# Retention and SwiGLU on one core: the first two chunks as pairs of batches, and an FFN that starts on half of its tokens

## The chip, the core and the metric

The kernel runs on one core of a Trainium2 chip, from one launch. The metric is the device time of that core in microseconds (us); lower is better. Of the two timed runs of the kernel before, one took 251.46 us and one, which was disturbed, 474.38 us; the comparisons in this document leave disturbed runs out. The profile is one execution of the same program, with a span of 248.7 us.

A core has four engines that matter here. TensorE multiplies matrices and writes its results to PSUM, a small memory of eight banks. VectorE and ScalarE read PSUM and write SBUF, the working memory. GpSimd works on SBUF alone, and can also issue transfers that change the type on the way. Sixteen DMA engines carry the transfers.

## What is computed

The inputs q, k and v have 4 batches, 8 heads, 768 positions and 64 numbers a head. The first half of the reference is a recurrence over the positions:

```python
gamma = 1.0 - 2.0 ** (-5.0 - np.arange(H))
for t in range(S):
    state = gamma * state + k[t] (outer) v[t]      # 64x64 for each batch and head
    y[:, :, t] = scale * q[t] @ state
```

Then the 8 heads of a position are laid side by side, which makes 3072 tokens of 512 numbers, and each token goes through a gated FFN with inner width 1536:

```python
rms = np.sqrt(np.mean(x * x, axis=-1, keepdims=True) + 1e-06)
xn = x / rms * rms_g
g = xn @ w_gate
silu = g * (1.0 / (1.0 + np.exp(-g)))
val = xn @ w_val
return silu * val @ w_out
```

The kernels don't step through the positions one by one. They cut the 768 positions into six chunks of 128. Inside a chunk the scores q k are multiplied by a causal mask and applied to v; what came earlier enters through the state, which is carried from chunk to chunk. The decay is folded into a factor on v and one on y.

## The kernel before

Six chunks follow one another. While the FFN of chunk c runs on all 512 tokens of the four batches, the attention of chunk c + 1 is worked off in slots between its matmuls. Each batch has its pieces: transposes (t), scores (a), y, norm (n) and transposes of the normed tokens (x).

The order of the first chunk is written out, and the FFN starts when all four batches are through it:

```python
for step in ("C0 T0 V0 W0 A0 T1 V1 Y0 W1 A1 T2 V2 Y1 W2 N0 A2 T3 X0 V3 Y2 W3 S0 N1 A3 S1 X1 Y3 N2 X2 S2").split():
    P[step[0]](0, int(step[1]))
...
warm_up(3)
piece_s(3)
piece_n(0, 3)
piece_x(0, 3)
warm_up(2)
```

The inputs of a batch and chunk come with one position on a partition, so a row of a transfer is 64 numbers of four bytes. Most are loaded by the sync queue as float32 and cast on GpSimd; those of chunk 0, batches 1 to 3, are cast in the transfer:

```python
x = loads.tile([128, H, D], F32, name=name)
i = nc.sync.dma_start(out=x, in_=src[b].rearrange("h (c p) d -> c p h d", p=C)[c])
...
nc.gpsimd.tensor_copy(qb, q_f.rearrange("p h d -> p (h d)"))
nc.gpsimd.tensor_copy(kb, k_f.rearrange("p h d -> p (h d)"))
nc.gpsimd.tensor_tensor(out=vp, in0=v_f, in1=vdec[:, c, :, None].to_broadcast([128, H, D]), op=ALU.mult)
```

From chunk 2 on, q and k are transposed by DMA, before that by TensorE. The scores and y of one batch:

```python
for hp in range(NHP):                      # 4 pairs of heads
    for i in range(2):
        r = slice(i * 64, i * 64 + 64)
        nc.tensor.matmul(a_ps[i][:, hp, :], d["kT"][r, hp, :], d["qT"][r, hp, :], start=True, stop=True)
for i in range(2):
    nc.vector.tensor_tensor(out=am[:, i], in0=a_ps[i], in1=causal..., op=ALU.mult)
...
# y: 8 matmuls of 64 columns, then the state part: 4 of 128 columns
nc.tensor.matmul(y_ps[:, h, :], d["am"][:, i, hp, :], d["vp"][:, h, :], ...)
nc.tensor.matmul(y_ps[:, 2 * hp:2 * hp + 2, :], d["qT"][:, hp, :], st_b[b][:, hp, :], ...)
# the addition to the state: 4 of 128 columns
nc.tensor.matmul(kv_ps[:, hp, :], d["kb"][:, sl], d["vp"][:, 2 * hp:2 * hp + 2, :], start=True, stop=True)
```

After these, VectorE scales y (x), ScalarE squares it, GpSimd adds and takes the power -0.5 (ms, rstd), VectorE norms (xn), and TensorE or a DMA transposes. The FFN, with four PSUM banks (fps) of its own:

```python
def gv(n):                                 # n of 12: 8 matmuls of 512 columns
    for s in range(KS):
        nc.tensor.matmul(g_ps, wg_b[:, s, sl], xnT[:, s, :], start=s == 0, stop=s == KS - 1)
    for s in range(KS):
        nc.tensor.matmul(v_ps, wv_b[:, s, sl], xnT[:, s, :], start=s == 0, stop=s == KS - 1)
    nc.scalar.activation(sg, g_ps, AF.Silu)
    nc.vector.tensor_tensor(out=hT[:, n, :], in0=sg, in1=v_ps, op=ALU.mult)

def down(b, n0=0, n1=NFF):                 # 12 matmuls of 512 columns for a batch
    for n in range(n0, n1):
        nc.tensor.matmul(o_ps, hT[:, n, b * C:(b + 1) * C], wo_b[:, n, :], ...)
    nc.scalar.copy(o_sb, o_ps)
    nc.sync.dma_start(out=out_v[c, b], in_=o_sb)
```

Of the kernel before, what the change touches and what calls it, by code (L numbers as in the profile page):

```python
# [11 lines left out]
AX = mybir.AxisListType  # L12
# [5 lines left out]
def kernel(  # L18
# [15 lines left out]
    C = 128  # L34
# [11 lines left out]
    loads = ctx.enter_context(tc.tile_pool(name="loads", bufs=8))  # L46
    work = ctx.enter_context(tc.tile_pool(name="work", bufs=3))
    ffw = ctx.enter_context(tc.tile_pool(name="ffw", bufs=3))
    aps = ctx.enter_context(tc.tile_pool(name="aps", bufs=4, space=bass.MemoryType.PSUM))
    fps = ctx.enter_context(tc.tile_pool(name="fps", bufs=4, space=bass.MemoryType.PSUM))  # L50


    out_v = out.rearrange("(b c p) m -> c b p m", b=B, p=C)

    SYNC_DEP = mybir.DependencyInfo(mybir.DependencyClass.Sync, mybir.DependencyReason.DATA)


    raw = {}

    def load(c, b, after=None):  # L60
        t = []
        for name, src in (("q_f", q), ("k_f", k), ("v_f", v)):
            x = loads.tile([128, H, D], F32, name=name)
            i = nc.sync.dma_start(
                out=x, in_=src[b].rearrange("h (c p) d -> c p h d", p=C)[c])
            if after is not None:
                tc.add_manual_dep(i.ins, after.ins.name, SYNC_DEP, reason="transfer order")
            t.append(x)
        raw[c, b] = t

    raw0 = {}

    def load0(b):
        for name, src in (("qb", q), ("kb", k)):
            x = work.tile([128, DM], BF16, name=name, bufs=6)
            nc.gpsimd.dma_start(
                out=x.rearrange("p (h d) -> p h d", h=H),
                in_=src[b].rearrange("h (c p) d -> c p h d", p=C)[0])  # L80
            raw0[name, b] = x
        x = loads.tile([128, H, D], F32, name="v_f")
        nc.gpsimd.dma_start(out=x, in_=v[b].rearrange("h (c p) d -> c p h d", p=C)[0])
        raw0["v", b] = x

    load(0, 0)
    g_col = const.tile([128, KS], F32, name="g_col")
    with nc.allow_non_contiguous_dma(reason="one column per 128 entries"):
        nc.scalar.dma_start(out=g_col, in_=moe_rms_g.rearrange("(s p) -> p s", p=128))


    pos_i = const.tile([128, NCH], mybir.dt.int32, name="pos_i")
    nc.gpsimd.iota(pos_i, pattern=[[C, NCH]], base=1, channel_multiplier=1)

    lngs = const.tile([128, H], F32, name="lngs")
    for h in range(H):
# [5 lines left out]
    pos_f = const.tile([128, NCH], F32, name="pos_f")  # L102
    nc.vector.tensor_copy(pos_f, pos_i)
    darg = const.tile([128, NCH, H], F32, name="darg")
    nc.vector.tensor_tensor(
        out=darg, in0=pos_f[:, :, None].to_broadcast([128, NCH, H]),
        in1=lngs[:, None, :].to_broadcast([128, NCH, H]), op=ALU.mult)
    vdec = const.tile([128, NCH, H], F32, name="vdec")
    ydec = const.tile([128, NCH, H], F32, name="ydec")
    nc.scalar.activation(vdec, darg, AF.Exp, scale=-1.0, bias=zero)  # L110
    nc.scalar.activation(ydec, darg, AF.Exp, scale=1.0, bias=lnscale)

    warm = const.tile([128, 1], F32, name="warm")
    nc.scalar.activation(warm, zero, AF.Silu)
    mhalf = const.tile([128, 1], F32, name="mhalf")
    nc.vector.memset(mhalf, -0.5)
    ident = const.tile([128, 128], BF16, name="ident")
    make_identity(nc, ident)
    causal = const.tile([128, 128], BF16, name="causal")
    nc.gpsimd.memset(causal, 1.0)  # L120
    nc.gpsimd.affine_select(
        out=causal, in_=causal, compare_op=ALU.is_ge, fill=0.0, base=0,
        pattern=[[1, 128]], channel_multiplier=-1)
    for b in range(1, B):
        load0(b)

    g_bc = const.tile([128, DM], F32, name="g_bc")

    st_f = [const.tile([128, NHP, 2 * D], F32, name=f"st_f{b}") for b in range(B)]
    st_b = [const.tile([128, NHP, 2 * D], BF16, name=f"st_b{b}") for b in range(B)]
    for b in range(B):
        nc.vector.memset(st_b[b], 0.0)


    wg_b = const.tile([128, KS, DFF], BF16, name="wg_b")
    wv_b = const.tile([128, KS, DFF], BF16, name="wv_b")
    wo_b = const.tile([128, NFF, DM], BF16, name="wo_b")
    wg_v = moe_w_gate.rearrange("(k p) n -> p k n", p=128)  # L140
    wv_v = moe_w_val.rearrange("(k p) n -> p k n", p=128)
    wo_v = moe_w_out.rearrange("(n p) m -> p n m", p=128)
    WB = 384

    landed = {}

    def load_w(i):
        sl = slice(i * WB, (i + 1) * WB)
        nc.gpsimd.dma_start(out=wg_b[:, :, sl], in_=wg_v[:, :, sl])
        landed["w", i] = nc.gpsimd.dma_start(out=wv_b[:, :, sl], in_=wv_v[:, :, sl])  # L150

    def load_wo(i):
        sl = slice(i * 4, (i + 1) * 4)
        landed["wo", i] = nc.gpsimd.dma_start(out=wo_b[:, sl, :], in_=wo_v[:, sl, :])


    cur = {}

    def piece_c(b):
        q_f, k_f, v_f = raw.pop((0, b))  # L160
        for name, x in (("qb", q_f), ("kb", k_f)):
            raw0[name, b] = work.tile([128, DM], BF16, name=name, bufs=6)
            copy = nc.vector.tensor_copy if name == "qb" else nc.scalar.copy
            copy(raw0[name, b], x.rearrange("p h d -> p (h d)"))
        raw0["v", b] = v_f

    def piece_v(b):
        vp = work.tile([128, H, D], BF16, name="vp", bufs=6)
        nc.vector.tensor_tensor(
            out=vp, in0=raw0["v", b], in1=vdec[:, 0, :, None].to_broadcast([128, H, D]), op=ALU.mult)  # L170
        cur[0, b]["vp"] = vp

    def cast(c, b):
        q_f, k_f, v_f = raw.pop((c, b))
        qb = work.tile([128, DM], BF16, name="qb", bufs=6)
        kb = work.tile([128, DM], BF16, name="kb", bufs=6)
        vp = work.tile([128, H, D], BF16, name="vp", bufs=6)
        nc.gpsimd.tensor_copy(qb, q_f.rearrange("p h d -> p (h d)"))  # L178
        nc.gpsimd.tensor_copy(kb, k_f.rearrange("p h d -> p (h d)"))  # L179
        nc.gpsimd.tensor_tensor(  # L180
            out=vp, in0=v_f, in1=vdec[:, c, :, None].to_broadcast([128, H, D]), op=ALU.mult)
        cur[c, b] = dict(qb=qb, kb=kb, vp=vp)
        if c > 1:
            d = cur[c, b]
            for n in "qk":
                t = work.tile([128, NHP, 128], BF16, name=n + "T", bufs=6)
                nc.sync.dma_start_transpose(out=t, in_=d[n + "b"])
                d[n + "T"] = t

    def piece_t(c, b):  # L190
        if c > 1:
            return
        if c == 0:
            cur[c, b] = dict(qb=raw0["qb", b], kb=raw0["kb", b])
        d = cur[c, b]
        qk_ps = aps.tile([128, 2, NHP, 128], BF16, name="qk_ps", tag="at")
        for i, n in enumerate(("qb", "kb")):
            for hp in range(NHP):
                nc.tensor.transpose(qk_ps[:, i, hp, :], d[n][:, hp * 128:(hp + 1) * 128], ident)  # L199
        qkT = work.tile([128, 2, NHP, 128], BF16, name="qkT")  # L200
        if c == 0 and b in (0, B - 1):
            nc.scalar.copy(qkT[:, 0], qk_ps[:, 0])
            nc.vector.tensor_copy(qkT[:, 1], qk_ps[:, 1])
        else:
            nc.scalar.copy(qkT, qk_ps)
        d["qT"] = qkT[:, 0]
        d["kT"] = qkT[:, 1]

    def piece_a(c, b):
        d = cur[c, b]  # L210
        a_ps = [aps.tile([128, NHP, 128], F32, name=f"a_ps{i}", tag="at") for i in range(2)]
        for hp in range(NHP):
            for i in range(2):
                r = slice(i * 64, i * 64 + 64)
                nc.tensor.matmul(a_ps[i][:, hp, :], d["kT"][r, hp, :], d["qT"][r, hp, :],  # L215
                                 start=True, stop=True)
        am = work.tile([128, 2, NHP, 128], BF16, name="am")
        for i in range(2):
            nc.vector.tensor_tensor(  # L219
                out=am[:, i], in0=a_ps[i],  # L220
                in1=causal[:, None, :].to_broadcast([128, NHP, 128]), op=ALU.mult)
        d["am"] = am

    def piece_y(c, b):
        d = cur[c, b]
        y_ps = aps.tile([128, H, D], F32, name="y_ps", tag="at")
        first = True
# [34 lines left out]
    def piece_s(b):  # L262
        nc.scalar.copy(st_f[b], cur[0, b]["kv"])
# [187 lines left out]
```

## Time and profile before

| What | Value |
|---|---|
| time of the undisturbed run | 251.46 us |
| span of the profile | 248.7 us |
| TensorE busy | 225.9 us |
| VectorE / ScalarE / GpSimd busy | 128.1 / 87.4 / 95.2 us |
| DMA packets | 108213, 35.94 MB |
| first matmul of any kind | 5.20 us |
| first matmul of FFN 0, 1, 2 | 24.38, 65.43, 104.53 us |
| first matmul of FFN 3, 4, 5 | 141.29, 178.10, 213.59 us |

In the page, a group of instructions has its line in the kernel, the engine, the operation, the tile that it writes and those it reads, a count, busy time, the mean duration of one in ns, and the idle time ahead of it with what ended it. PE is TensorE, PEld its loading of weights, DVE VectorE, ACT ScalarE, POOL GpSimd. A matmul's mean is its latency from start to end; in a stream the next starts before the last has ended, so spacing is read from the order of time. The slices cut the span into 40 equal parts of 6.2 us with a digit of busy tenths for each.

### The profile page before, as it was taken

The page shows a single profiled execution, that of the slowest core. Times are in us where ns is not written, and L with a number is a line of the kernel's source. Part 1 is how long each engine was busy: PE and PEld are TensorE (multiplying, and loading weights), DVE is VectorE, ACT ScalarE, POOL GpSimd, SP SyncE. Part 2 cuts the span into 40 slices and gives each one's busy share as a digit, 9 for nine tenths or more (in the row PEclk, how much of TensorE's full clock was granted, in tenths as well). Part 3 has the DMA queues.
Part 4 walks back from the last instruction along what each step waited for, and adds up shares of the span by engine and source line. Part 5 has one row for each costly group of instructions (what it writes and reads, how often), then busy time and mean ns, then how long its engine had stood idle before and what let it go on. Part 6 is the DMA issues. An engine that isn't in the chain of part 4 may idle for free.

```text
span 248.7 us, 4121 instructions
## 1 busy us (share of the span) xinstructions
PE 225.9 (91%) x1495; PEld 114.4 (46%) x1521; DVE 128.1 (51%) x215; ACT 87.4 (35%) x170; POOL 95.2 (38%) x177
## 2 busy tenths in 40 slices
PE   1776999979996989999989999989999999999993
PEld 0553445545433545445544445544444444444443
DVE  4796337676234895036894046894047781134300
ACT  6365334531431242232342322433232422332221
POOL 8978144953850236910246910246900211000000
PEclk9997999999999999999999999999999999999999
DMA  9999999898997699955999356999453114200022
GB/s 140 174 195 203 196 219 221 151 199 167 218 290 109 144 222 189 229 127 87 213 209 175 127 131 98 199 207 209 122 115 66 21 21 129 86 0 0 0 87 86
DMA packets 108213, 35.94 MB, mean 145 GB/s; under 512 B 99040, under 2 KB 104928, under 8 KB 108192
## 3 DMA queue, kind: packets, MB, share of 16 engines
q1 hardware_dynamic: 95232, 29.24, 60.8%
q0 software_dynamic: 12288, 6.29, 19.0%
q8 instruction: 12, 0.20, 0.3%
q10 hardware_dynamic: 672, 0.13, 0.3%
q14 instruction: 9, 0.07, 0.1%
HBM read 28.58 MB, written 6.29 MB: 140 GB/s over the span
## 4 chain that ended last, share of the span: by engine, by line
PE 77%; DVE 10%; DMA 5%; issue 3%; ACT 3%; POOL 0%; SPq 0%; DVEq 0%; ACTq 0%
PE o_ps L361 24%; PE v_ps L338 21%; PE g_ps L335 21%; DVE am L219 4%; PE a_ps L215 3%; PE y_ps L232 2%; DMA v_f<-in_v_dram 2%; DVE x L247 2%; DMA k_f<-in_k_dram 2%; PE kv_ps L244 1%; PE y_ps L237 1%; DMA kT<-kb 1%; DVE xn L283 1%; PE o_ps L351 1%; PE qk_ps L199 1%
## 5 line engine op out<-in xcount | busy, mean ns | idle before, releaser
L341 DVE TENSOR_TENSOR hT<-sg,v_ps 128x512 bf16<-128x512 bf16 x72 | 49.4, 687 | 89.6 <-PE v_ps L338 83.2
L338 PE MATMUL v_ps<-xnT,wv_b 128*128 128x512 bf16 x282 | 73.4, 379 | 0.5
L335 PE MATMUL g_ps<-xnT,wg_b 128*128 128x512 bf16 x276 | 72.9, 380 | 0.4
L340 ACT ACTIVATE sg<-g_ps 128x512 bf16<-128x512 f32 x72 | 42.8, 594 | 63.7 <-PE g_ps L335 62.2
L361 PE MATMUL o_ps<-wo_b,hT 128*128 128x512 bf16 x269 | 60.8, 379 | 1.2 <-DMA wo_b<-in_moe_w_out_dram 0.8
L338 PEld LDWEIGHTS <-wv_b 128*128 128x128 bf16 x288 | 28.2, 98 | 34.0
L335 PEld LDWEIGHTS <-wg_b 128*128 128x128 bf16 x288 | 26.6, 98 | 31.5 <-issue 0.9
L361 PEld LDWEIGHTS <-hT 128*128 128x128 bf16 x276 | 26.6, 98 | 30.9 <-issue 0.8
L272 POOL TENSOR_SCALAR ms<-ssq 128x1 f32<-128x1 f32 x24 | 4.5, 189 | 92.4 <-ACT xsq L251 92.3
L251 ACT ACTIVATE xsq<-x 128x512 f32<-128x512 f32 x24 | 15.1, 630 | 48.7 <-DVE x L247 48.6
L219 DVE TENSOR_TENSOR am<-a_ps,causal 128x512 bf16<-128x512 f32 x48 | 30.8, 682 | 2.4 <-PE a_ps L215 2.4
L366 ACT COPY o_sb<-o_ps 128x512 f32<-128x512 f32 x23 | 13.5, 585 | 36.8 <-PE o_ps L361 30.7
L180 POOL TENSOR_TENSOR vp<-v_f,vdec 128x512 bf16<-128x512 f32 x20 | 20.7, 1037 | 3.4 <-DMA v_f<-in_v_dram 3.4
L268 POOL CAST st_b<-st_f 64x256 bf16<-64x256 f32 x40 | 17.3, 432 | 1.3
L247 DVE TENSOR_TENSOR x<-y_ps,ydec 128x512 f32<-128x512 f32 x24 | 16.4, 685 | 1.4 <-PE y_ps L237 0.8
L232 PE MATMUL y_ps<-vp,am 128*128 128x64 bf16 x192 | 12.0, 200 | 5.4 <-DVE am L219 5.1
L178 POOL CAST qb<-q_f 128x512 bf16<-128x512 f32 x20 | 12.1, 606 | 8.7 <-DMA q_f<-in_q_dram 7.9
L283 DVE SCALAR_TENSOR_TENSOR xn<-x,rstd,g_bc 128x512 bf16<-128x512 f32 x16 | 12.5, 784 | 5.5 <-POOL rstd L275 5.5
L232 PEld LDWEIGHTS <-am 128*128 128x128 bf16 x192 | 9.2, 101 | 13.1 <-DVE am L219 9.7
L275 POOL TENSOR_TENSOR rstd<-ms,mhalf 128x1 f32<-128x1 f32 x24 | 13.2, 552 | 2.0
L179 POOL CAST kb<-k_f 128x512 bf16<-128x512 f32 x20 | 12.2, 609 | 2.6 <-DMA k_f<-in_k_dram 1.7
L259 DVE TENSOR_TENSOR st_f<-st_f,kv_ps 128x512 f32<-128x512 f32 x16 | 10.8, 676 | 0.0
(60 smaller groups left out, 125.5 us busy)
## 6 DMA issues: line engine op xcount, KB each, us to landing
out_dram<-o_sb SPq DMA_DIRECT2D x23, 256.0 KB, 2.2
q_f<-in_q_dram SPq DMA_DIRECT2D x21, 256.0 KB, 4.8
k_f<-in_k_dram SPq DMA_DIRECT2D x21, 256.0 KB, 5.0
v_f<-in_v_dram SPq DMA_DIRECT2D x21, 256.0 KB, 5.1
wg_b<-in_moe_w_gate_dram POOLq DMA_DIRECT2D x4, 384.0 KB, 9.6
wv_b<-in_moe_w_val_dram POOLq DMA_DIRECT2D x4, 384.0 KB, 10.7
wo_b<-in_moe_w_out_dram POOLq DMA_DIRECT2D x3, 512.0 KB, 8.3
v_f<-in_v_dram POOLq DMA_DIRECT2D x3, 256.0 KB, 6.2
```

The lines of the kernel that those rows point to most:

```text
L180: nc.gpsimd.tensor_tensor(out=vp, in0=v_f, in1=vdec[:, c, :, None].to_broadcast([128, H, D]), op=ALU.mult)
L219: nc.vector.tensor_tensor(out=am[:, i], in0=a_ps[i], in1=causal[:, None, :].to_broadcast([128, NHP, 128]), op=ALU.mult)
L232: nc.tensor.matmul(y_ps[:, h, :], d["am"][:, i, hp, :], d["vp"][:, h, :], start=first, stop=last, skip_group_check=True)
L247: nc.vector.tensor_tensor(out=x, in0=y_ps, in1=ydec[:, c, :, None].to_broadcast([128, H, D]), op=ALU.mult)
L251: nc.scalar.activation(xsq, x.rearrange("p h d -> p (h d)"), AF.Square, accum_out=ssq)
L268: nc.gpsimd.tensor_copy(st_b[b][r, :, i * 64:i * 64 + 64], st_f[b][r, :, i * 64:i * 64 + 64])
L283: nc.vector.scalar_tensor_tensor(out=xn, in0=x, scalar=d["rstd"], in1=g_bc, op0=ALU.mult, op1=ALU.mult)
L335: nc.tensor.matmul(g_ps, wg_b[:, s, sl], xnT[:, s, :], start=s == 0, stop=s == KS - 1)
L338: nc.tensor.matmul(v_ps, wv_b[:, s, sl], xnT[:, s, :], start=s == 0, stop=s == KS - 1)
L340: nc.scalar.activation(sg, g_ps, AF.Silu)
L341: nc.vector.tensor_tensor(out=hT[:, n, :], in0=sg, in1=v_ps, op=ALU.mult)
L361: nc.tensor.matmul(o_ps, hT[:, n, b * C:(b + 1) * C], wo_b[:, n, :], start=n == 0, stop=n == NFF - 1)
```

## The change

Three things change together.

1. Chunks 0 and 1 are worked in pairs of batches. Two neighbouring positions lie on one partition, 64 partitions for each batch of the pair, so that a row of a transfer is 128 numbers. The matmuls of a pair use quadrants of the array: 64 rows by 64 columns (scores, kv), or 64 rows by 128 (y). In chunk 0 the decay sits in a float32 mask, so that y needs no scaling after it.
2. The FFN of chunk 0 starts when the first pair is through: five of its twelve steps run on 256 tokens first, and on the other 256 later. The rest of chunk 0, its state and the whole of chunk 1 are written out, step by step, between FFN 0's steps.
3. From chunk 2 on, a pair of batches takes two visits to TensorE: the scores of both, then y, state part and kv of both. The FFN and attention have four PSUM banks each. q and k are cast in the transfer by GpSimd, one addition updates the state of a pair, and ScalarE's queue issues the stores.

The core of the diff, cut (the rest spells out the order of steps):

```diff
-    load(0, 0)
-    ...                       # sync queue, float32, rows of 64
+    pair_v = {n: s.rearrange("b h (c j e) d -> c b j h (e d)", c=NCH, e=2) for n, s in srcs.items()}
+    def load_pair(c, p, n, eng=None, f32=False, after=None):
+        ...
+        for b in range(2):
+            i = (eng or nc.gpsimd).dma_start(out=x[b * 64:b * 64 + 64], in_=pair_v[n][c, 2 * p + b])
+    def load(c, b, names="qkv"):            # chunks 2 to 5: cast in the transfer
+        ...
+            x = work.tile([128, DM], BF16, name=n + "b", bufs=8)
+            nc.gpsimd.dma_start(out=x.rearrange("p (h d) -> p h d", h=H), in_=unit_v[n][c, b])

-                nc.tensor.matmul(a_ps[i][:, hp, :], d["kT"][r, hp, :], d["qT"][r, hp, :], ...)
+    def ap(c, p, a):                        # twice a pair: 16 matmuls of 128 columns, 64x64 quadrants
+        ...
+                        nc.tensor.matmul(ps[i][t, o:o + 128], kt[r, x, b, e], qt[r, x, b], start=True, stop=True)
+    def kvp(c, p):                          # once a pair: 32 matmuls of 64 columns, 64x64 quadrants
+        ...
+                        nc.tensor.matmul(u["kv"][b][t, hp * D:hp * D + D], u["k"][r, h, s], u["vp"][r, h, s], ...)
+    def y0(p, a):                           # twice a pair: 16 matmuls of 64 columns, 64 rows
+        ...
+                        nc.tensor.matmul(u["y"][b][:, h * D:h * D + D], u["am", a, i][r, x, e, :],
+                                         u["vb"][r, h, e * D:e * D + D], ...)

+    def values(c, p):                       # chunks 2 to 5, both batches of a pair
+        ...                                 # state part: 16 matmuls of 64 columns, 64 rows
+                    nc.tensor.matmul(ys[i][:, o:o + D], U[c, b]["qT"][r, hp, :], st_b[p][r, j, hp, :], ...)
+        ...                                 # kv: 16 of 64 columns on 64 columns of the array
+                        nc.tensor.matmul(kv[i * 64:i * 64 + 64, o:o + D], U[c, b]["k"][:, h * D:h * D + D],
+                                         U[c, b]["vp"][:, h, :], start=True, stop=True)
+        ...                                 # y: 16 of 64 columns

+    def gv(c, n0, n1, t0, t1):              # steps n0 to n1, tokens t0 to t1
+    ...
+    gv(0, 0, 1, 0, 256)
+    ...
+    norm0(1)
+    gv(0, 3, 4, 0, 256)
+    vp_pair(0, 1)
+    kvp(0, 0)
+    x_pe(0, 1, 0)
+    ...
+    gv(0, 0, 2, 256, 512)

-            nc.scalar.copy(o_sb, o_ps)
-            nc.sync.dma_start(out=out_v[c, b], in_=o_sb)
+        nc.scalar.copy(o_sb, ps)
+        store(nc.scalar, c, b, slice(0, DM), o_sb)

+                1: [L(values, d, 0), L(vp, d, 2), L(vp, d, 3)],
+                2: [L(y_out, d, 0, 0)],
+                5: [L(a_pair, d, 1), L(norm, d, 0, 0), L(x_dma, d, 0, 0)] + ...,
+                6: [L(norm, d, 0, 1), L(x_dma, d, 0, 1), L(a_mask, d, 2, 0)] + ...,
+                9: [L(values, d, 1)],
+                13: [L(a_pair, d + 1, 0), L(a_mask, d + 1, 0, 0, 1), L(a_mask, d + 1, 1, 0, 1)] * more,
```

In the last part a number is a step of chunk c's FFN (0 to 11 are gv, 12 to 15 down), d is c + 1, and the list is what follows that step.

## The prediction

> **What bounds the kernel now.** I read the page's busy table first, then the slices, the costliest groups, the windows by stage, and the order of TensorE's work where the windows showed a loss.
>
> ```profile
> PE 225.9 (91%) x1495; PEld 114.4 (46%) x1521; DVE 128.1 (51%) x215; ACT 87.4 (35%) x170; POOL 95.2 (38%) x177
> PE   1776999979996989999989999989999999999993
> DMA  9999999898997699955999356999453114200022
> ```
>
> TensorE is busy 91% of a 248.7 us span, no other engine over 51%. The slices say where the 22.8 us without it lie: mostly in the first four, a little in slices 9, 13 and 15, and in the last one. The DMA row below it is full in the same first slices.
>
> ```profile
> L338 PE MATMUL v_ps<-xnT,wv_b 128*128 128x512 bf16 x282 | 73.4, 379 | 0.5
> L335 PE MATMUL g_ps<-xnT,wg_b 128*128 128x512 bf16 x276 | 72.9, 380 | 0.4
> L361 PE MATMUL o_ps<-wo_b,hT 128*128 128x512 bf16 x269 | 60.8, 379 | 1.2 <-DMA wo_b<-in_moe_w_out_dram 0.8
> ```
>
> A mean of 379 ns is latency, not spacing. The chain of waits merges four such matmuls into 0.86 us, so one costs 216 ns in a stream. The FFN of a chunk is 96 + 48 = 144 of them: 31.1 us, six times 186.7 us. The change can't touch this.
>
> Stage by stage, from one FFN's first matmul to the next (the order of TensorE's work gives the cuts, the windows the busy time):
>
> ```profile
> 0.00:24.38 24.38, 14.11 (x133) 9.44 (x135) 17.09 (x42) 14.04 (x30) 20.38 (x39) 0.93 1.38 178
> 24.38:65.43 41.05, 38.80 (x285) 20.20 (x288) 22.54 (x36) 15.22 (x27) 21.58 (x40) 1.00 1.10 194
> 65.43:104.53 39.10, 35.74 (x237) 17.62 (x240) 20.58 (x32) 12.05 (x24) 18.34 (x33) 1.00 1.04 200
> 104.53:141.29 36.76, 35.63 (x236) 17.64 (x240) 20.49 (x32) 12.05 (x24) 14.78 (x29) 1.00 0.88 162
> 141.29:178.10 36.81, 35.69 (x238) 17.64 (x241) 20.49 (x32) 12.06 (x24) 14.78 (x29) 1.00 0.91 158
> 178.10:213.60 35.50, 34.80 (x222) 16.73 (x225) 18.19 (x28) 12.05 (x24) 5.34 (x12) 1.00 0.32 75
> 213.60:248.70 35.10, 31.10 (x154) 15.14 (x155) 8.68 (x13) 9.88 (x17) 0.00 (x0) 1.00 0.11 38
> ```
>
> Columns: window, its length, then busy us (and instructions) of TensorE, its weight loads, VectorE, ScalarE and GpSimd, then clock, DMA share, GB/s. What exceeds 31.1 us is attention of the next chunk, waits, or the tail: 10.0, 8.0, 5.7, 5.7, 4.4 and 4.0 us. Ahead of them stand 24.4 us with no FFN at all.
>
> How much of the 5.7 us of a middle chunk is work? In the order of TensorE's work one batch takes 0.33 us for the scores (a_ps), 0.23 for y, 0.22 for the state part, 0.22 for kv and 0.10 in between: 1.10, four times 4.4. The remaining 1.2 us is one place in each chunk:
>
> ```profile
> 129.67 0.20 PE L232 MATMUL y_ps<-vp,am 128*128 128x64 bf16 x1 [0.47 <-DVE am L219]
> 130.27 0.38 PE L232 MATMUL y_ps<-vp,am 128*128 128x64 bf16 x7 [0.40 <-DVE am L219]
> ```
>
> The last batch's y waits for its two masks on VectorE. Chunk 2 has another, besides that one:
>
> ```profile
> 76.51 0.40 PE L215 MATMUL a_ps<-qT,kT 64*128 64x128 bf16 x8 [2.28 <-DMA kT<-kb]
> ```
>
> **What the Trainium skill says.** *DMA: Bandwidth & Descriptors*, section Why small descriptors are slow (HBM only), charges each packet a fixed overhead, 27% at 256 bytes. The trace agrees in kind: 99040 of 108213 packets are under 512 bytes, and the plain hardware queue's 95232 packets took 60.8% of 16 engines' 248.7 us, 25 ns each for 307 bytes on average. *TensorE: Matmul & The Clock Gate*, section Wait — 56ns, not 53.3ns?, puts a floor of some 25 ns between the starts of small matmuls. The trace has about 30 ns between 64-column matmuls when warm (the seven y_ps at 19.33 us end 0.38 us later, one lasts 0.20). No run here shows yet whether four quadrants go below that. *TensorEngine Tiling (Array Packing)*, section Key Properties, says that a switch of tiling mode drains the array; the 0.10 us between kv and the next a_ps agrees. *TensorE: Matmul & The Clock Gate*, section Part 1: The HAM clock gate, has a cold array at half rate: the seven y_ps at 9.95 us take 0.56 us, some 55 ns apart, as that says.
>
> **The change part by part.**
>
> *The front.* Now TensorE has its first input at 5.20 us and the first FFN matmul at 24.38, because all four batches go through scores, masks, y, squares, norm and transposes in turn. The changed kernel runs two batches through this and starts FFN on 256 tokens. I walk that chain with the durations of before: q there at about 5 us (its first 256 KB landed at 4.25); two casts at 0.90; transposes and copies (0.6 and 0.42 each, partly beside each other) to about 9.0; scores 0.9; four masks at 0.68 to 12.4; ScalarE meanwhile four more exponentials, the cast of v (a 1024-wide pass was 1.00) and four small exponentials; y to about 13.9; squares 0.8 and the table load 1.28; power 0.56; norm 0.8; transposes and copy 1.5. That gives 18 to 19.5 us; I take 18.5, 5.9 us earlier than now.
>
> *What this moves behind it.* Batches 2 and 3 of chunk 0 and all state updates now lie inside FFN 0, together with chunk 1. In pairs these are more, smaller matmuls: 64-row, 64-column quadrants. Behind the first FFN matmul and ahead of FFN 1 I count y 32, kv 4 x 32, transposes of q and k 2 x 32, scores 2 x 32, y of chunk 1 2 x 32: 352 small ones at 28 ns, 9.9 us; 32 full ones (xn transposes, state part) at 56 ns, 1.8 us; 14 switches at 0.1, 1.4 us. With 31.1 for the FFN the second FFN starts at 18.5 + 31.1 + 13.1 = 62.7 if nothing waits. I add 1.0 for the array cold at its start and waits: 63.7 against 65.43, **1.7 us gained**. Most of the 5.9 us is given back, since the work was only moved and in part cut smaller.
>
> *Loads of chunks 0 and 1.* 24 loads of 1024 rows of 256 bytes become as many bytes in rows of 512: 12288 packets fewer. At up to 25 ns over 16 engines that is up to 19 us of DMA time, realistically half, in slices where the DMA row is 9. It makes the earlier start possible; it is not a gain of its own.
>
> *Casts in the transfer.* 40 GpSimd casts of q and k (24.3 us) and most of the 40 state casts (17.3 us) leave. In come 83 instead of 20 DMA issues on GpSimd at 0.75 to 0.95, some 54 us more. GpSimd's busy time grows from 95 to about 115 us, and up to FFN 1 it has 47 issues (41 us), four 1024-wide products at about 2.1 and small work: some 55 of 64 us.
>
> *Chunks 2 to 5.* Scores of a pair 16 x 28 ns, state part, kv and y the same, with five switches: 2.3 us a pair, 4.6 a chunk against 4.4. No gain in work; masks are now a step or more ahead of their use, so the 1.2 us wait goes. FFN 1 carries the 0.55 us of chunk 1's last xn transposes and 0.65 of chunk 3's first scores: 31.1 + 4.6 + 1.2 = 36.9, **2.2 gained**, since the 2.28 us wait for kT should go with the earlier load. FFN 2 and 3: 35.7, **1.1 each**. FFN 4 has no kv and its first scores are done: 33.9, **1.6**. FFN 5 and the tail: the same.
>
> *Sum.* 1.7 + 2.2 + 1.1 + 1.1 + 1.6 = 7.7: a span of 241.0 us. The undisturbed run of before took 251.46 us for a span of 248.7, so I add 2.8: **243.8 us**, 3.0% less.
>
> **The rivals.** *Quadrants cost what full matmuls cost.* If the 64-column weight loads keep small matmuls 56 ns apart, 352 of them cost 9.9 us more in front and some 64 a chunk 1.8 us more: about 17 us, 260 us. Against it: 64-row matmuls run at half the spacing here already. *Quadrants really run side by side*, at 14 ns: about 5 us less in front, 3 later: 236. *GpSimd's queue takes TensorE's place as the bound in front.* It works in order: the products of v stand behind waits for the power, and chunk 1's loads behind the products. By my walk the first kv would wait some 2 us and a later one as long: 247 to 249, "same". For it speaks the 55 of 64 us; against it the ready weights. *Transfers were the true limit in front.* wo lands just in time now (TensorE waits 0.79 us at 51.2). If software transfers of 256-byte rows are slower than hardware ones, chunk 2 and wo come late and the gain of the front is lost: 246 to 250. *ScalarE*, which now issues the stores at 0.33 us each, has room (12 of 37 us).
>
> **Range and chances.** The middle chunks' 6 us are the safest; the front can be anything from 5 us better to 4 worse, and quadrants add either way. I give 236 to 251 for 8 in 10. Faster by over 2% means under 246.4, which needs two thirds of the sum: 0.66. Within 2%: 0.26. Slower, only with the first rival or a blocked queue: 0.08.
>
> **What would show it.** First FFN matmul at 18 to 19.5 us; FFN 1 starting at 62 to 66; windows of 36 to 37, 35 to 36 twice, then 34; no wait of y for masks in chunks 2 to 5; small matmuls about 28 ns apart; GpSimd busy over 105 us. I am wrong if TensorE waits for kv's operand, for weights or for q and k of chunks 1 and 2, or if the spacing of quadrants is far from 28 ns.

## Result: 262.5 us, slower, and where the time came from

The changed kernel takes 262.53 us (two runs, 262.35 and 262.71). Its ratio to the kernel before is 1.0434, with a 95% interval of 1.0389 to 1.0479: 4% slower, where 3% faster had been predicted. The span of the profiled run went from 248.7 to 260.4 us.

First the page of the changed kernel, the busy table and the slices, to be held against the same rows of before:

```profile
PE 233.9 (90%) x2034; PEld 126.1 (48%) x2034; DVE 126.9 (49%) x220; ACT 87.1 (33%) x176; POOL 116.0 (45%) x154
PE   7679499799937999979899999799999999999994
...
PEclk9999979999986999999999999999999999999999
DMA  8999469999996975999699799299650102500022
```

TensorE is still the busy engine and no other is above 49%. Its row has two holes that before didn't have: a 4 in slice 5 (26 to 33 us) and a 3 in slice 12 (72 to 78 us). With each of them the row PEclk, the share of its clock that TensorE was granted, dips (7 in slice 6, 8 and 6 in slices 12 and 13). In the kernel before that row dips once, in front:

```profile
PEclk9997999999999999999999999999999999999999
```

Where TensorE runs at half its clock it is called cold below, as in the prediction. TensorE's busy time grew by 8 us although the FFN work is the same: in part it has more small matmuls to do, in part the same ones at half clock.

Stage by stage, cut at the first FFN matmul of each chunk (window, its length, busy us and instructions of TensorE, weight loads, VectorE, ScalarE, GpSimd, then clock, DMA share, GB/s):

```profile
19.96:69.94 49.98, 44.93 (x568) 27.02 (x568) 24.57 (x48) 16.64 (x36) 38.87 (x47) 0.97 1.22 162
69.94:116.74 46.80, 38.79 (x367) 24.82 (x362) 26.41 (x39) 14.13 (x30) 24.11 (x30) 0.93 1.06 137
116.74:153.88 37.14, 35.52 (x272) 16.84 (x273) 20.44 (x30) 11.25 (x23) 22.70 (x28) 1.00 1.26 126
```

| stage | predicted | before | changed | changed minus predicted |
|---|---|---|---|---|
| up to the first FFN matmul | 18.5 | 24.38 | 19.96 | +1.5 |
| FFN 0 | 45.2 | 41.05 | 49.98 | +4.8 |
| FFN 1 | 36.9 | 39.10 | 46.80 | +9.9 |
| FFN 2 | 35.7 | 36.76 | 37.14 | +1.4 |
| FFN 3 | 35.7 | 36.81 | 37.40 | +1.7 |
| FFN 4 | 33.9 | 35.50 | 34.32 | +0.4 |
| FFN 5 and tail | 35.1 | 35.10 | 34.80 | -0.3 |
| span | 241.0 | 248.7 | 260.4 | +19.4 |

The earlier start is there (4.4 us). FFN 0 and FFN 1 together, where 14.7 of the 19.4 us of error lie, are 16.6 us longer than before. The order of TensorE's work (start, us, instruction; in brackets how long TensorE had stood still and who ended it) names the largest places:

```profile
30.43 0.45 PE L305 MATMUL kv_ps<-vp,k2b 64*64 64x64 bf16 x32 [3.21 <-POOL vp L276]
...
47.09 0.45 PE L305 MATMUL kv_ps<-vp,k2b 64*64 64x64 bf16 x32 [1.40 <-POOL vp L276]
...
79.57 1.87 PE L531 MATMUL g_ps<-xnT,wg_b 128*128 128x256 bf16 x8 [5.96 <-ACT sg L535]
```

Two waits for GpSimd's product of v, 4.6 us, and one of 5.96 us for an activation of ScalarE. An engine that is busy 33% of the span held up one that is busy 90%. ScalarE's own order of work says how:

```profile
69.75 0.59 ACT L552 COPY o_sb<-o_ps 128x512 f32<-128x512 f32 x1 [3.69 <-PE y_ps L384]
75.28 2.38 ACTq L543 DMA_DIRECT2D out_dram<-o_sb  x2
77.71 0.63 ACT L425 ACTIVATE xsq<-x 128x512 bf16<-128x512 f32 x1 [7.37 <-DMA kT<-kb]
```

From 70.3 to 77.7 us ScalarE computes nothing. Ahead of it in its own queue stand the two halves of FFN 0's last store, and the second of them is issued only when kT, a transpose of chunk 2 issued by SyncE, has landed. The data have nothing to do with each other. By the trace's semaphores each half waits on the completion semaphore that a transpose used last: the first half on that of the qT issued at 66.94 us, which landed at 75.21, the second on that of kT. Eight such semaphores serve the hardware transfers of both queues in this trace, SyncE's and ScalarE's, so that a transfer of one queue can hold up the other. That kT was slow:

```profile
68.30 2.13 SPq L450 DMA_TRANSPOSE kT<-kb  x1
```

It was issued at 68.30 and landed at 77.2, 8.9 us later. The Trainium skill, *DMA: Bandwidth & Descriptors*, section Anatomy of one DMA — SWDGE (gpsimd) path, says that transfers don't wait for semaphores themselves; the sequencer of the issuing engine does, before it dispatches. That section is about transfers that GpSimd issues; the trace shows the same of these stores, which are ScalarE's. The 7.37 us above are that: whatever stands behind the store in ScalarE's program waits with it.

GpSimd's order of work shows the other loss:

```profile
27.81 0.70 POOL L346 TENSOR_TENSOR rstd<-ms,mhalf 128x2 f32<-128x2 f32 x1 [6.46 <-DVE ms L341]
28.49 1.89 POOL L276 TENSOR_TENSOR vp<-v2f,vd_p 128x1024 bf16<-128x1024 f32 x1
```

GpSimd stood still for 6.46 us in front of the second pair's power, with the product that TensorE needed right behind it in the program.

### The profile page after: what moved, and what is told of

It is laid out like the page before. It is cut to its first block, busy times and chain, and to the rows that moved or that the text cites. A ratio compares the mean times of both kernels' runs of the same rounds, so it can differ in the third digit from the quotient of the medians.

```text
span 260.4 us, 5059 instructions
## 1 busy us (share of the span) xinstructions
PE 233.9 (90%) x2034; PEld 126.1 (48%) x2034; DVE 126.9 (49%) x220; ACT 87.1 (33%) x176; POOL 116.0 (45%) x154
## 3 DMA queue, kind: packets, MB, share of 16 engines
q0 software_dynamic: 51248, 16.00, 59.3%
## 4 chain that ended last, share of the span: by engine, by line
PE 54%; DMA 16%; DVE 10%; POOL 7%; issue 6%; ACT 4%; ACTq 0%; SPq 0%; DVEq 0%; POOLq 0%
PE o_ps L550 17%; PE g_ps L531 16%; PE v_ps L531 15%; DMA kT<-kb 8%; DMA v2f<-in_v_dram 5%; DVE hT L536 3%; ACT xsq L425 2%; DVE x L416 2%; DMA out_dram<-o_sb 2%; DVE xn L436 2%; POOL vp L276 2%; PE a_ps L459 2%; PE y_ps L504 2%; POOL k2b L99 1%; DVE am L468 1%
## 5 line engine op out<-in xcount | busy, mean ns | idle before, releaser
L536 DVE TENSOR_TENSOR hT<-sg,v_ps 128x512 bf16<-128x512 bf16 (+1 forms) x75 | 49.6, 664 | 95.8 <-PE v_ps L531 53.6
L531 PE MATMUL g_ps<-xnT,wg_b 128*128 128x512 bf16 (+1 forms) x340 | 77.4, 358 | 8.0 <-ACT sg L535 6.0
L531 PE MATMUL v_ps<-xnT,wv_b 128*128 128x512 bf16 (+1 forms) x340 | 77.2, 357 | 0.3 <-DMA wv_b<-in_moe_w_val_dram 0.3
L535 ACT ACTIVATE sg<-g_ps 128x512 bf16<-128x512 f32 (+1 forms) x75 | 42.9, 577 | 77.7 <-PE g_ps L531 76.5
L425 ACT ACTIVATE xsq<-x 128x512 bf16<-128x512 f32 x20 | 12.4, 621 | 25.5 <-DVE x L416 15.8
L442 POOL TENSOR_TENSOR vp<-v_f,vd_n 128x512 bf16<-128x512 f32 x16 | 17.9, 1155 | 0.0
L112 POOL DMA_DIRECT2D qb<-in_q_dram x16 | 15.0, 938 | 0.2 <-issue 0.2
L112 POOL DMA_DIRECT2D kb<-in_k_dram x16 | 14.4, 899 | 0.8 <-DMA wo_b<-in_moe_w_out_dram 0.8
L109 POOL DMA_DIRECT2D v_f<-in_v_dram x16 | 14.7, 916 | 0.0
L416 DVE TENSOR_TENSOR x<-y_ps,yd_n 128x512 f32<-128x512 f32 x16 | 10.6, 684 | 1.1 <-PE y_ps L504 1.1
```

The lines of the kernel that those rows point to most:

```text
L109: nc.gpsimd.dma_start(out=x, in_=unit_v[n][c, b])
L112: nc.gpsimd.dma_start(out=x.rearrange("p (h d) -> p h d", h=H), in_=unit_v[n][c, b])
L416: nc.vector.tensor_tensor(out=x[:, :, :, i, :], in0=u["y"][i].rearrange("p (b a d) -> p b a d", b=2, a=NHP), in1=yd_n[:, c, i][:, None, :, ...
L425: nc.scalar.activation(xsq, u["x"][:, b], AF.Square, scale=1.0 / math.sqrt(DM), accum_out=ms[:, b:b + 1])
L442: nc.gpsimd.tensor_tensor(out=x, in0=U[c, b]["v"], in1=vd_n[:, c, :, None].to_broadcast([128, H, D]), op=ALU.mult)
L531: nc.tensor.matmul(x[:, o:o + w], wt[:, s, n * 128:(n + 1) * 128], XT[c][:, s, t0:t1], start=s == 0, stop=s == KS - 1)
```

## The experiments

Theory: **A**, ScalarE's stand-still behind the shared completion semaphore, and **D**, GpSimd's order in front, are two separate losses on TensorE's path; what is left are steps that stand at the wrong place (**S**). Rivals: **B**, the transfers themselves are too slow (the transposes of q and k land 5.5 and 7.0 us after issue, 2.4 in the kernel before), so that any wait removed comes back as a wait for data; and **T**, the software transfers cause that (48 ns a packet: 59.3% of 16 engines over 260.4 us, for 51248 packets). The expectations of the first three runs have rivals of their own; in them C says that it is the issuing on ScalarE that costs. All ratios are to the kernel before on the same chip.

### Stores of FFN 0 on SyncE's queue

```
-        store(nc.scalar, c, b, slice(0, DM), o_sb)
+        store(nc.sync if c == 0 else nc.scalar, c, b, slice(0, DM), o_sb)
```

> The changed kernel with one edit: the stores of FFN 0 are issued by the sync queue, not by ScalarE's. Theory A (a store on ScalarE's queue waits until DMA transposes of chunk 2, which use the same completion semaphores, have landed; ScalarE then stands still, and with it the activations and TensorE): the wait of 5.96 us in FFN 1 and the 2 us of cold clock behind it go; FFN 1 shrinks from 46.8 to about 38.5 us, the time from 262.5 to about 254.5. Rival B (the loads of chunk 2 leave GpSimd's queue too late, ScalarE's wait only stands in front of another one): TensorE waits for kT at the first scores of chunk 2 instead, and the time stays above 260. Rival C (it is the issuing on ScalarE that costs): the same gain as A here, none in the run that keeps the stores on ScalarE.

Measured: 255.09 us, ratio 1.0155 (1.008 to 1.0229), 7.4 us less than the changed kernel. The window of FFN 1:

```profile
69.43:109.43 40.00, 36.90 (x362) 23.84 (x361) 25.98 (x39) 13.30 (x29) 22.94 (x29) 1.00 1.49 155
```

It fell from 46.80 to 40.00 us, and its clock rose from 0.93 to 1.00: with the wait of 5.96 us also the cold matmuls behind it went. kT still landed about 10 us after its issue, and TensorE, which needs it later than ScalarE had stopped for it, waited 1.23 us. So the loss was not that kT was late, but that ScalarE stood behind it.

### Stores left on ScalarE, transposes behind them

The four transposes of chunk 2's first pair are issued only when FFN 0's last store has landed, so ScalarE can't stand behind them.

```
     ...                             # t_dma takes a transfer to wait for; store keeps its last one
-    t_dma(2, 0)
-    t_dma(2, 1)
     load(2, 2)
     load(2, 3)
     down(0, 3)
+    t_dma(2, 0, last_store[0])      # each waits for the last store of down(0, 3)
+    t_dma(2, 1, last_store[0])
```

> The changed kernel with the stores of FFN 0 left on ScalarE's queue, but the DMA transposes of chunk 2's first pair made to wait for the last of these stores, so that no store waits for a transpose. Theory A: ScalarE goes on, the 5.96 us wait in FFN 1 goes, about 255 us; the transposes come some 3 us later, which may cost up to 1 us at the first scores of chunk 2. Rival B: above 260, with TensorE waiting for kT. Rival C: no gain, 262.

Measured: 264.35 us, ratio 1.0545 (1.0475 to 1.0614). ScalarE's wait is gone, but the time did not fall. TensorE's order of work:

```profile
82.25 0.40 PE L461 MATMUL a_ps<-qT,kT 64*128 64x128 bf16 x8 [1.21 <-DMA kT<-kb]
89.08 0.61 PE L461 MATMUL a_ps<-qT,kT 64*128 64x128 bf16 x8 [6.43 <-DMA kT<-kb]
```

The transpose was issued at 79.9 instead of 68.3 us and again took some 9 us to land, so TensorE itself now waits for it. This isn't a refutation of A (the stand-still went, and a delay of 11.6 us was put in its place), but it shows what B is worth: a transpose needs 9 us here, and must be issued that much ahead of its use. The rival C of the expectations also foresaw no gain here. The trace decides against it: with the stores still on ScalarE's queue ScalarE is back at work at 71.07 us, 1.77 us after its copy for the last of them, and what TensorE waits for is kT.

### GpSimd's order in front

```
-    vp_pair(0, 0)                      # stood behind power(0, 1)
-    for p in range(2): nc.gpsimd.memset(st_d[p], 0.0)
...
-    vp_pair(0, 1)
...
     load_w(5, 8)
+    vp_pair(0, 0)
+    vp_pair(0, 1)                      # now ahead of power(0, 1); the memsets behind load_w(1, 2)
```

> The changed kernel with GpSimd's order alone changed: the two products of v of chunk 0 stand ahead of the power of the second pair, and the clearing of the state tiles ahead of the power of the first pair, where GpSimd had waited 6.46 and 4.52 us. Theory D (TensorE's wait of 3.21 us for kv's operand in FFN 0, the cold clock behind it and the later 1.40 us are an order in GpSimd's queue): FFN 0 shrinks from 50.0 to about 43.5 us. What stands behind in GpSimd's queue comes some 5 us earlier, so that ScalarE's wait in FFN 1 stays about as long as it was: 256 us. Rival E (GpSimd's queue is full in front): the waits turn up at other places, 260 to 263.

Measured: 258.06 us, ratio 1.0269 (1.0201 to 1.0338), 4.5 us less than the changed kernel, where 6.5 had been expected. TensorE's waits for the product of v are gone, but FFN 0 lasts 46.1 us, not 43.5, and ScalarE's stand-still did not stay as it was: in the run profiled here, the longest of the four with 262.04 us, TensorE waits 8.43 us for it instead of 5.96. Not all of the front was won: the second pair's normalized values come when they came before, and TensorE waits for them instead, as the profile of the next kernel, which has this edit too, shows in TensorE's order of work:

```profile
28.59 1.03 PE L366 MATMUL x_ps<-ident,xn 128*128 128x128 bf16 x8 [2.19 <-ACT xn L353]
```

### Both edits

> The changed kernel with both edits already tried alone: the stores of FFN 0 on SyncE's queue, and on GpSimd's queue the two products of v behind the power and the loads of weights instead of ahead of them. Theory: ScalarE's stand-still ahead of FFN 1 and the waits of the kv matmuls for GpSimd are two independent losses, one behind the other on TensorE's path, worth 7.1 and 4.4 us alone, so together 262.5 - 11.5 = 251.0 us; FFN 1 starts at 66 us and lasts 40. Rival: the second only moves time into the first (FFN 1's start was 3.9 us earlier and ScalarE's wait 2.5 us longer in the run of the order alone), and what is left behind both is the landing of the loads, so no better than 254.5.

The expectation has the direction of the second edit the wrong way round: the two products of v come to stand ahead of the second pair's power, as in the run before.

Measured: 250.21 us, ratio 0.9952 (0.9926 to 0.9979). The sum held (251.0 expected), so A and D add up. FFN 1 starts at 65.99 us and lasts 39.78.

### The loads of v of chunks 2 to 5 on the hardware queue

```
-                nc.gpsimd.dma_start(out=x, in_=unit_v[n][c, b])
+                nc.sync.dma_start(out=x, in_=unit_v[n][c, b])
```

> The kernel of e5 with the 16 loads of v of chunks 2 to 5 on SyncE's hardware queue instead of GpSimd's software queue; same bytes, same rows, no other edit. Theory: the software transfers (48 ns a packet against 25 to 30 on the hardware queue) are what makes the transposes of q and k land 5.5 to 7 us after issue instead of 2.4, so with 16384 packets fewer in software the landing falls to 3 to 5 us and TensorE's waits for kT (about 1.2 in FFN 1, 1.4 in FFN 2, 0.4 in FFN 3) go: 248 us against 251. GpSimd's busy time doesn't fall (issues aren't counted), but its queue has 15 us less to do. Rival: the landing is set by the transposes themselves, one behind the other on SyncE, and v's loads in that queue only put 16 more issues ahead of them: waits for kT of 1 to 3 us stay, 251 to 253.

Measured: 249.72 us, ratio 0.9967 (0.9944 to 0.999), the same as without it. The queues and the landings of this kernel (packets, MB, share of 16 engines; then issues, median us to landing), below them the same rows of the kernel with both edits:

```profile
q0 software_dynamic: 49968, 11.80, 56.7%
q1 hardware_dynamic: 46704, 13.25, 32.2%
...
kT<-kb SPq DMA_TRANSPOSE x16, 5.7
```

```profile
q0 software_dynamic: 51248, 16.00, 63.4%
q1 hardware_dynamic: 30064, 9.05, 24.8%
...
kT<-kb SPq DMA_TRANSPOSE x16, 7.2
```

The step "16384 packets fewer in software" was wrong: only 1280 went, for 4.2 MB. The trace has them as 1024 packets of 4096 bytes and 256 of 4 bytes, where the hardware queue moves the same loads in 16640, 16384 of them of 256 bytes. The transfer engines were about as busy either way: the two shares add to 88.2% with both edits and to 88.9% here. The expectation that GpSimd's busy time doesn't fall was wrong too: the profile counts its issues as busy, and with 16 of them fewer it fell from 116.3 to 102.2 us. kT landed 1.5 us sooner, as T had it, and the wait for kT in FFN 1 (0.55 us) went; one of 0.31 for a bank came. The time didn't move.

### Steps moved

```
-  name="o_sb", bufs=3          +  bufs=4
   # middle chunks, step: what is emitted behind that FFN step
-  1: values(d, 0)              +  1: values(d, 0), y_out(d, 0, 0)
-  2: y_out(d, 0, 0)            +  2: y_out(d, 0, 1), squares, load(d+1, 1)
-  3: y_out(d, 0, 1), squares   +  3: state_add(d, 0)
-  4: state_add(d, 0)
-  5: a_pair(d, 1), ...         +  6: a_pair(d, 1), ...
-  9: values(d, 1)              +  9: values(d, 1), y_out(d, 1, 0)
- 10: y_out(d, 1, 0 and 1)      + 10: y_out(d, 1, 1)
- 12: load(d+2, 0), t_dma(..)   + 12: t_dma(..)      15: load(d+2, 0)
   # in FFN 1 likewise; in front gv(0, 4, 5, 0, 256) ahead of the second pair's x_pe
```

> The kernel of e5 with its order of steps mended, all transfers on the queues they had: y out and the adding of the state a step earlier, the second pair's scores a step later, the transposes of the next chunk ahead of the loads of the chunk after it, one FFN step put ahead of the second pair's xn transposes in front, FFN 1's scores and xn transposes a step later, four buffers for o_sb instead of three. Theory: the waits left in chunks 2 to 5 (0.3 to 0.8 for a bank that the adding of the state frees, 0.58 for the last hT, 0.4 to 1.4 for kT, 1.3 for o_sb) come from where steps stand, not from what they cost; they go, the middle windows fall from 37.3 to 35.5, FFN 1 to 38, and the time to 246. Rival: the resources are full (VectorE, the transfers), each wait comes back at another place: 250 to 251.

Measured: 245.89 us, ratio 0.9798 (0.9753 to 0.9842), as expected. The windows of FFN 1 to 3:

```profile
66.58:104.78 38.20, 36.61 (x362) 23.95 (x361) 25.95 (x39) 13.28 (x29) 22.25 (x28) 1.00 1.28 152
104.78:140.04 35.26, 35.05 (x268) 16.74 (x273) 19.27 (x30) 11.70 (x24) 22.24 (x27) 1.00 1.66 143
140.04:175.23 35.19, 34.98 (x270) 16.75 (x272) 19.41 (x30) 11.84 (x24) 15.12 (x19) 1.00 1.02 133
```

In the middle windows TensorE is busy all but 0.2 us. What had been lost there are these lines of the changed kernel's order of work, which are absent now:

```profile
129.77 0.38 PE L459 MATMUL a_ps<-qT,kT 64*128 64x128 bf16 x7 [0.84 <-DVE st_f L510]
...
145.22 2.98 PE L550 MATMUL o_ps<-wo_b,hT 128*128 128x512 bf16 x13 [0.58 <-DVE hT L536]
```

The scores of the second pair waited for a bank of PSUM which the adding of the state had to empty first, and the down projection for the last hT, which VectorE did behind two outputs of y. Both are order, not capacity, since they went with the same work done. How much each of the moves, or the fourth buffer, is worth by itself was not tried.

### Steps moved and v by hardware

> The kernel of e7 and v's loads of chunks 2 to 5 on the hardware queue, as in e6. If order and transfers each take away waits of their own: 243.5 us, near what the prediction gave for the change (its middle windows were 35.7, FFN 1 36.9). If the waits for kT are gone in e7 already: the same as e7, 246. If neither helps: 251.

Measured: 246.32 us, ratio 0.9805 (0.9758 to 0.9852): nothing beyond the moved steps. kT now lands 3.3 us after issue, against 5.5 with the moved steps alone, and it doesn't matter, since the moved steps leave TensorE only 0.26 us of waiting for it. The second of the three outcomes.

### The front in another order, and warmed

```
     ap_mask(0, 1, 0, 1)
+    ap_mask(0, 1, 1, 0); ap_mask(0, 1, 1, 1)
     gv(0, 0, 1, 0, 256)
-    ap_mask(0, 1, 1, 0); ap_mask(0, 1, 1, 1)
     load_w(5, 8)
-    vp_pair(0, 0); vp_pair(0, 1); gv(0, 1, 2, 0, 256)
-    y0(1, 0); y0(1, 1); gv(0, 2, 3, 0, 256)
+    vp_pair(0, 0); y0(1, 0); y0(1, 1); gv(0, 1, 2, 0, 256)
     squares0(1); eps0(1); power(0, 1)
+    vp_pair(0, 1)
     norm0(1)
+    gv(0, 2, 3, 0, 256)
     gv(0, 3, 4, 0, 256)
```

> The kernel of e7 with the front in another order: VectorE does all four masks of the second pair before the first product of the FFN, y of the second pair follows the first FFN step instead of the second, and on GpSimd the power stands between the two products of v instead of behind both. Theory: the 2.19 us that TensorE still waits in front come from a chain that only starts late (masks to 23.6, y, squares, power at 27.3, xn at 28.0 to 28.7), and the array is cold for some 1.2 us more after it; the chain starts some 1.5 to 2 us earlier, so the wait goes, FFN 1 starts at 63.5 to 64.5 instead of 66.6 and the time is 242.5 to 243.5 us against 245.9. Rival: the transfers set the front (weights for FFN steps 2 and 3 land just then, as the 0.54 us wait for wv in the run of v by hardware hints); the wait turns into one for weights and FFN 1 starts at 66 to 66.6 as before, 245.5.

Measured: 244.05 us, ratio 0.972 (0.9653 to 0.9787). FFN 1 starts at 64.82 us, 1.8 earlier, a little short of what was expected. The wait didn't go, it shrank from 2.19 to 1.61 us:

```profile
27.60 0.51 PE L305 MATMUL kv_ps<-vp,k2b 64*64 64x64 bf16 x32 [1.61 <-ACT xn L353]
```

kv doesn't read xn; it waits for the banks that y held until xn was made from it. The chain to xn began 2 us sooner, but VectorE has the second hT, whose operand comes at 24.27 us, in its queue ahead of the statistics of y, and xn came at 26.86 to 27.6 instead of 28.0 to 28.7. No wait for weights took its place, so the rival of this run falls.

```
+            for _ in range(hot if name == "g_ps" else 0):     # hot=2 in the first gv
+                nc.tensor.matmul(x, ones[:, :128], ones, start=True, stop=True)
```

> The kernel of e9 with two 512-column matmuls on the constant ones ahead of the first FFN matmul, in the 0.67 us in which TensorE waits for the copy of xnT; their result is overwritten. If the cold clock of the first four FFN groups (0.85 us each instead of 0.44) comes from this gap alone, they run warm and about 1.2 us are gained: 241.5 us. If the array is cold from the thin work of the 7 us before, the two matmuls themselves run at half rate, 0.86 us for a gap of 0.67, and the time is the same as e9 or 0.2 more.

Measured: 243.35 us, ratio 0.9671 (0.9602 to 0.9739). TensorE's order of work from the two added matmuls on:

```profile
18.94 1.06 PE L529 MATMUL g_ps<-ones 128*128 128x512 bf16 x2
19.82 1.03 PE L533 MATMUL g_ps<-xnT,wg_b 128*128 128x256 bf16 x4
20.65 1.06 PE L533 MATMUL v_ps<-xnT,wv_b 128*128 128x256 bf16 x4
21.64 1.04 PE L291 MATMUL y_ps<-vb,am 64*128 64x64 bf16 x32
22.61 0.75 PE L533 MATMUL g_ps<-xnT,wg_b 128*128 128x256 bf16 x4
23.20 0.60 PE L533 MATMUL v_ps<-xnT,wv_b 128*128 128x256 bf16 x4
```

They run cold themselves (0.88 us for two) and so do the first FFN groups behind them; at 23 us, 4 us after dense work began, the groups are at 0.44 us. So the first expectation falls: this gap alone isn't what makes the array cold. What the second says of the two matmuls holds. Filling the gap still lets the array warm up sooner, and FFN 1 starts 0.37 us earlier; that the time is 0.7 us lower than without them can't be told from no difference, since the intervals overlap.

The version with the two matmuls is 3.3% faster than the kernel before and, by the two ratios (0.9671 to 1.0434), 7.3% faster than the change as it came. It has every part of the change in it.

### In the kernel before: scores of the last batch a step earlier

```
-    PLAN = dict(..., a=(4, 6, 8, 10), y=(6, 8, 10, 12), ...)
+    PLAN = dict(..., a=(4, 6, 8, 9), y=(6, 8, 10, 12), ...)
```

> The kernel before with one edit: from chunk 2 on the scores of the last batch stand one step earlier (9 for 10), so that its masks have a step more before y. The prediction took 0.87 us a chunk as what the change gains by spreading the masks. If that holds: four times 0.87, about 248 us against 251.5 (ratio 0.986). Rival F: VectorE has no room for the masks earlier, or PSUM banks are short, and the wait turns up elsewhere: within 0.5 us of before.

Measured: 247.98 us, ratio 0.9874 (0.9817 to 0.9931). The waits of y for its masks are gone, and the windows of FFN 2 and 3 are 35.54 and 35.55 us, 1.2 less than before. That is the 1.2 us a chunk that the prediction gave for this wait; the 0.87 in the expectation is the two gaps of the trace alone. FFN 0 and FFN 1 are 0.9 and 0.4 us longer in this profile, with a cold TensorE at FFN 0's start and behind the wait for kT. The prediction read that wait rightly, and one digit in the kernel before takes it away without the rest of the change.

## Why the prediction was wrong, point by point

**The first FFN matmul at 18.5 us (18 to 19.5): nearly.** 19.96 us, just outside; the walk along the chain was 1.5 us short.

**The count of small matmuls: right. Their cost: too high.** Between the two starts TensorE ran exactly 384 of them, the 352 and 32 counted. They took some 9.8 us with all switches, not 13.1. The term that was off is "28 ns each": 32 kv quadrants go by in 0.38 us, 12 ns each with the switch, while 16 transposes take 0.47, 29 ns each. The rival that quadrants run side by side was right for quadrants. The Trainium skill has both statements: the floor of 25 ns from which the prediction reasoned, and, in *TensorE: Matmul & The Clock Gate*, section Part 3: Packing small matmuls — row/col tiling, that tiles at different positions in the array run at the same time, their starts some 4 ns apart. The second is the one that holds for four quadrants. The trace has mostly 3 to 4 ns between the starts of four kv matmuls, one in each quadrant, and some 22 ns before the next four: 8 ns on average, and about 32 ns until the same quadrant comes again.

**"I add 1.0 for the array cold at its start and waits": the step that failed in FFN 0.** Waits were 3.21 + 1.40 + 0.33 = 4.94 us, cold matmuls about 4.1 (the first four FFN groups and the y behind them 2.2, the groups behind the wait of 3.21 us and the one at 24.58 1.9). That is 9.0 us for the term of 1.0; with 31.1 for the FFN and 9.8 for the small work it makes 49.9 of 49.98 us. The prediction had named the wait, as its rival of GpSimd's queue, with "some 2 us and a later one as long", and TensorE waiting for kv's operand was its first sign of being wrong; it was right in kind and nearly in size, and was given too little weight. What the rival did not have is the clock: from 32 to 35 us, behind the wait of 3.21 us, the granted clock is 0.50.

**FFN 1 at 36.9 us: the largest error, and no rival had it.** 46.80 = 31.1 + 6.1 of small work (5.8 predicted) + 8.0 of waits (5.96 for ScalarE, 1.34 for o_sb, 0.38 and 0.32) + 1.6 cold. The step that failed is the sentence that ScalarE "has room (12 of 37 us)". Room is a statement on busy time; a queue in order stops at its first unmet wait, however little it has to do. The run with the stores on SyncE shows it: the same work, 7.4 us less. The 2.28 us wait for kT, which was to go, became 0 here and 1.23 us once ScalarE was out of the way.

**FFN 2 and 3 at 35.7: right in work, wrong in waits.** 37.14 = 31.1 + 4.4 of small work (4.6 predicted) + 1.6 of waits. The wait for masks did shrink (0.20 left), but a bank (0.84) and the last hT (0.58) came in its place; in FFN 3 it was kT (1.31) and the last hT (0.58). With the steps moved the windows are 35.2, below the prediction.

**FFN 4 and the tail: right** within 0.4 us.

**Rivals.** Full price for quadrants: wrong. Transfers as the true limit: the transposes do land later (7.0 instead of 2.4 us), and where they were issued 11.6 us later TensorE waited 6.43 us for one; but at their own places they cost 1.4 us a window at most (1.31 us in FFN 3 of the changed kernel; 1.23 and 1.41 in FFN 1 and 2 with the stores on SyncE), and a landing of 3.3 instead of 5.5 us with v by hardware changed nothing once the steps were moved. What this slow landing comes from is not settled; v's loads are a part of it, the loads of q and k with a cast were not tried by hardware.

**The sum.** A, D and S took 7.4, 4.9 and 4.3 us off, one after the other, and the order and warmth of the front 2.5: 262.5 to 243.35 us. The prediction's 243.8 is about what the last version takes, and its span of 241.0 compares with 241.8. That is no merit of the prediction, which was to say what this kernel does and had none of these edits in it. The agreement is partly chance: FFN 1 in the last version is 38.76 us, 1.9 over the prediction (waits of 0.90, 0.58 and 0.39), and the middle windows are 0.5 under it.

## What to carry to other kernels

Before a small instruction goes to an engine "with room", list what stands behind it in that engine's program, and what it may wait for, the completion semaphores that it shares with other transfers included: a store of half a microsecond stopped an engine for 7.4 us. A change that moves work early adds in-order queues to the path; walk each of them, not only TensorE's. A wait of TensorE of 2 us or more may have to be paid again in clock. It did not always: behind 2.28 us of waiting for kT in the kernel before the clock stayed at 1.00, and behind 2.30 us for the same kT, with the scores a step earlier, it was 0.50 for some 3 us and cost 1.6 us. When a good change measures slow, look at the windows before giving it up: four edits of order, queue and one more buffer, none of which changed what is computed, made 262.5 us into 244.1.

## What was not expected of the hardware

- 32 quadrant matmuls of 64 by 64 start 8 ns apart on average and are through in 0.45 us: mostly 3 to 4 ns within four that use the four quadrants, then some 22 ns. 16 transposes with an output of 64 rows take 0.64 us, 28 ns between starts.
- The loads of v as 32-bit numbers went as packets of 4096 bytes from the software queue and of 256 bytes from the hardware queue. The sum of both queues' transfer time hardly differed (88.2 and 88.9% of 16 engines). The software transfers that stayed, weights and loads with a cast for the most part, took 45 ns a packet (56.7% of 16 engines over 248.5 us, 49968 packets), against 25 ns on the hardware queue of the kernel before.
- The transposes of kT, from SBUF to SBUF and all of one size, landed between 2.4 and 13.0 us after their issue within the changed kernel (median 7.0).
- After the thin work in front TensorE stayed cold for a while after the first dense matmul: until 25 us in the changed kernel, 5 us after it, and until 23 us in the last version, 4 us after it. The row PEclk doesn't show this: it reads 9 there, while the groups of four take 0.85 us instead of 0.44. Behind the wait of 5.96 us the next 16 matmuls of 256 columns took 3.4 us instead of 1.75.
